# Moving sums, copies, scores and one store in a fused attention and feed-forward kernel

## The chip, the cores and the metric

One core of a Trainium2 chip runs the kernel in one launch. The metric is the device time of one execution in microseconds (us); less is better. The runs before took 310.1, 310.56 and 311.13; the median is 310.56.

## The reference

Eight batches of attention with 8 heads, 576 positions and 64 dimensions per head, with a decay bias, then a feed-forward layer (512 to 2048 to 512) over all 4608 tokens:

```python
scores = scale * np.matmul(q, k.transpose(0, 1, 3, 2))
s_pos = np.maximum(s, 0.0)
cum = np.cumsum(s_pos, axis=-1)
bias = -(cum[:, :, :, None] - cum[:, :, None, :])
scores = np.where(causal, -1000000000.0, scores + np.minimum(bias, 0.0))
attn = softmax(scores)
x = np.matmul(attn, v)      # then heads side by side: 4608 x 512
h = x @ w_in
out = (0.5 * h * (1.0 + erf(h / np.sqrt(2.0)))) @ w_out
```

## The kernel before

Batches pass through attention one after the other, and tokens pass through the feed-forward layer in nine chunks of 512. Chunk c's layers run on TensorE (PE) between the attention steps of batch c + 1, all in an order that is written out by hand: every engine executes its instructions in the order in which the code issues them, and waits only for data and for buffers. PE's results go to a few named PSUM slots: "m0" and "m1" of one bank each, "x", "y" and "z" of two banks each; a slot that is taken again waits for the readers of what it held.

Per batch, `tr_two`, `tr_one` (PE) transpose q and k into `qkT`, and VectorE or ScalarE copy the result out of PSUM; from batch 3 on DMA transposes do this. `sc_mm` makes the scores of a pair of heads in two units and ScalarE takes their exponential into `P`; `mask` multiplies by a triangle. `sc_first` is the form for batch 0: the mask is added by PE (`ident_bf` times `off_bf`), and the bank's first matmul opens the group. The decay is a weight `wb` = exp(cum) on the keys' side: `scale_v` (VectorE) scales V by it into `vv`, and PE forms denominators (`av_d`, weights `wb`) and sums (`av_o`, weights `vv`) with the same `P`. Then ScalarE takes a reciprocal by logarithm and exponential (`ln`), and VectorE multiplies into `xT`. For batch 0 this goes by halves of chunk 0, `av_first` and `x_first`; afterwards by `av_main` and `av_tails`.

`l1_first` and `l1_item` are layer 1 (`h_ps`, two 128-wide tiles at a time), followed on ScalarE by the activation into `gT`. Layer 2 is `l2_item` for chunk 0 (16 accumulating matmuls into `o_ps`, copied out and stored). For later chunks it is `prod`, seven products in place of eight, which need sums of `gT` (`sums`, into `gs`) and of the weights (`weight_sums`, into `w_sums`), all on VectorE. `fill` issues matmuls whose result nobody reads. `put` and `put_one` store a block of the output.

What stands around the places that change: batch 0's prefix sum `weights_dve` runs after the first tiles, and its transposes `weights_mm` after those of the first keys; `av_first(1, ...)` stands behind the first eight matmuls of layer 1; in chunk 1, `after(f2)` issues the transposes of batch 2 behind the chunk's sums; in the last chunk the store of the last block but one is issued by ScalarE:

```python
put(c, 1, 0, pb, m1, queue=nc.scalar)
for i in range(2):
    prod(c, 2, p2[i], more=True, subs=(i,), at=i)
    put_one(c, i, p2[i][:, 0])
```

Of the kernel before, what the change touches and what calls it, by code (L numbers as in the profile page):

```python
# [19 lines left out]
def kernel(  # L20
# [10 lines left out]
    nc = tc.nc  # L31
    fp32 = mybir.dt.float32
# [16 lines left out]
    FT = dff // 128  # L49
# [205 lines left out]
    def weight_sums(i):  # L255
# [8 lines left out]
        nc.vector.tensor_tensor(t[3], b21, t[1], op=ALU.subtract)  # L264

    cum = const.tile([64, S], fp32, name="cum")

    def weights_dve():
        s_pos = work.tile([64, S], fp32, tag="w64", bufs=1, name="s_pos")
        nc.scalar.activation(s_pos, s_sw, func=AF.Relu)  # L270
        nc.vector.tensor_tensor_scan(s_pos, one, s_pos, 0.0, op0=MULT, op1=ALU.add)
        nc.vector.tensor_scalar(cum, s_pos, s_pos[:, 287:288], None, op0=ALU.subtract)

# [174 lines left out]
    def sc_first(p, u, slot):  # L448

        if u == 0:  # L450
            P_of[0, p] = work.tile([128, 2, PW], bf16, tag="P", bufs=4, name="P")
        P = P_of[0, p]
        s_ps = bank(slot, [128, 2, 512], fp32, "sc_ps")
        for n_part, (jt, i0, n, off) in enumerate(UNITS[u]):
            for e in range(2):
                nc.tensor.matmul(
                    s_ps[:, e, off : off + n],
                    lhsT=qkT[0][e * 64 : e * 64 + 64, 1, p, jt * 128 : jt * 128 + 128],
                    rhs=qkT[0][e * 64 : e * 64 + 64, 0, p, i0 : i0 + n],
                    start=n_part == 0, stop=False, skip_group_check=True,  # L460
                )
        for e in range(2):
            nc.tensor.matmul(
                s_ps[:, e].rearrange("p (g c) -> p g c", c=256)[:, :, 0:128], lhsT=ident_bf,
                rhs=off_bf.unsqueeze(1).to_broadcast([128, 2, 128]),
                start=False, stop=True, skip_group_check=True,
            )
            if u == 1:
                nc.tensor.matmul(
                    s_ps[:, e, 448:512], lhsT=ident_bf, rhs=off_bf[:, 0:64],  # L470
                    start=False, stop=True, skip_group_check=True,
                )
        nc.scalar.activation(
            P[:, :, UO[u] : UO[u] + UW[u]], s_ps[:, :, : UW[u]], func=AF.Exp, scale=scale
        )
# [67 lines left out]

    def av_first(c, qds, d_ps, oo):

        for qd in qds:
            av_mm(0, qd, d_ps[:, qd], None, PART[c])
            for t in range(2):
                av_mm(0, qd, oo[:, qd, t], t, PART[c])

# [67 lines left out]

    def l2_item(c, sub, f0=0, f1=FT, slot=None, eng=None):

        gT = gT_of[c]
        if f0 == 0:
            if slot is None:
                o_of[c, sub] = bank(M[sub % 2], [128, KO * 128], fp32, "o_ps")
            elif slot in M:
                o_of[c, sub] = bank(slot, [128, KO * 128], fp32, "o_ps")
            elif sub == 2:
                two = bank(slot, [128, 2, KO * 128], fp32, "o_ps")
                o_of[c, 2], o_of[c, 3] = two[:, 0], two[:, 1]
        o_ps = o_of[c, sub]  # L630
        for ft in range(f0, f1):
            nc.tensor.matmul(  # L632
                o_ps, lhsT=gT[:, ft, sub * 128 : (sub + 1) * 128],
                rhs=w_out_r[:, ft], start=(ft == 0), stop=(ft == FT - 1),
            )
        if f1 < FT:
            return
        o_sb = work.tile([128, KO * 128], fp32, tag="osb", bufs=4, name="o_sb")
        copy(eng or nc.vector, o_sb, o_ps)
        r0 = c * NB + sub * 128  # L640
        nc.sync.dma_start(out=out[r0 : r0 + 128], in_=o_sb)
# [58 lines left out]

    def put(c, t, n, ps_, plus, eng=None, subs=slice(0, 2), queue=nc.sync):

# [6 lines left out]
        queue.dma_start(  # L709
            out=out[r0 : r0 + HC, n * HC : n * HC + HC].rearrange("(s p) x -> p s x", p=128)[:, subs],  # L710
# [70 lines left out]
    oo0 = bank(X, [128, 2, 2, 256], fp32, "av_o")  # L781
    av_first(0, (0, 1), d0, oo0)
    x_first(0, (0, 1), d0, oo0, ln0)
    sc_first(3, 1, Z)
    fill(f_ps, 6)
    scale_v(0, STS[4:5], nc.vector)
    for k0 in (0, 2):
        l1_first(0, 0, k0, k0 + 2)
    d1 = bank(M[1], [128, 2, 256], fp32, "av_d")
    oo1 = bank(X, [128, 2, 2, 256], fp32, "av_o")  # L790
    av_first(1, (0, 1), d1, oo1)
    for qd in range(2):
        x_first(1, (qd,), d1, oo1, ln1)
    l1_first(0, 1, 0, KO)
    for k0 in (0, 2):
# [19 lines left out]
    for c in range(NCH):  # L815
        nb = c + 1

        def after(f2):
            if c == 0:
# [48 lines left out]
        if c == 0:  # L868
# [43 lines left out]
        elif nb < B:  # L912
            exp_set()
            m1, u2, u3, u4, pa, pb, x, y, z = products(c, order[c])
            order[nb] = (y, x, z)
            sums(c, 7, 8, (0, 1))
            prod(c, 1, pa)
            nc.vector.tensor_copy(m1, pa)
            sums(c, 7, 8, (2,))
            sc_mm(nb, 0, (z, x))  # L920
            sc_mm(nb, 1, (y,))
# [60 lines left out]
        else:  # L982
# [188 lines left out]
```

## Time and profile before

| | |
|---|---|
| median of the runs | 310.56 us |
| profiled execution, its own time | 311.02 us |
| its span, first to last instruction | 309.1 us |
| granted PE clock, mean | 0.997 |
| busy: PE, VectorE (DVE), ScalarE (ACT) | 298.9, 229.2, 227.5 us |

In a timeline row stand the start and the length in us, the engine, the line in the code, the operation, output<-input by the program's names, shapes and count; in brackets the idle time before it and what ended it. PEld is PE's loading of weights, SPq, ACTq and POOLq are the queues from which DMAs are issued. Ends of matmuls are modelled: one is shown some 0.27 us long for 256 columns, but the next starts 0.11 later.

### The profile page before, as it was taken

To read this page: it belongs to the slowest core of one execution; us is meant where nothing else is said; L and a number is where in the kernel's file an instruction comes from. 1 tells how busy PE (TensorE), PEld (TensorE's weight loads), DVE (VectorE), ACT (ScalarE), POOL (GpSimd) and SP (SyncE) were. 2 spreads that over 40 slices of the span, in tenths; PEclk is the share of its full clock that TensorE was granted. 3 is DMA by queue.
4 is the path that set the end of the run, shared out by engine and by line. 5 is a ranking of instruction groups with operands and counts; after the bars stand their busy time and mean duration, and the time that the engine had idled before them with its cause. 6 is when DMAs were issued, how large, how long until landed. Compare 5 with 4: busy or idle time off the path is not lost.

```text
span 309.1 us, 8419 instructions
## 1 busy us (share of the span) xinstructions
PE 298.9 (97%) x3544; PEld 192.3 (62%) x3544; DVE 229.2 (74%) x513; ACT 227.5 (74%) x293; POOL 72.8 (24%) x97
## 2 busy tenths in 40 slices
PE   7999999999999999999999999999999999999992
PEld 2565444545894578458854885488547854874581
DVE  5659268978699769996997699778977874554650
ACT  3869757867887788879877987798788879565500
POOL 8583447510002520171017201630000000000000
PEclk9999999999999999999999999999999999999998
DMA  7999999997027994799699996997540220030013
GB/s 114 224 217 207 206 233 235 227 185 92 2 72 172 141 170 116 169 149 161 123 155 149 166 133 149 148 161 142 131 90 2 70 70 1 2 123 13 3 40 105
DMA packets 111692, 39.16 MB, mean 127 GB/s; under 512 B 95360, under 2 KB 109696, under 8 KB 111648
## 3 DMA queue, kind: packets, MB, share of 16 engines
q0 software_dynamic: 54992, 17.18, 50.2%
q1 hardware_dynamic: 56096, 20.86, 33.6%
q8 instruction: 29, 0.48, 0.7%
q10 hardware_dynamic: 560, 0.52, 0.5%
q14 instruction: 15, 0.12, 0.2%
HBM read 36.85 MB, written 9.44 MB: 150 GB/s over the span
## 4 chain that ended last, share of the span: by engine, by line
PE 75%; DMA 18%; POOL 3%; issue 1%; ACTq 1%; ACT 0%; DVE 0%; POOLq 0%
PE h_ps L608 33%; PE pb L682 14%; PE pa L682 9%; DMA raw_v<-in_v_dram 6%; DMA w_out_r<-in_moe_w_out_dram 5%; PE pd L682 5%; PE pe L682 5%; PE sc_ps L438 4%; DMA tok<-in_q_dram 4%; DMA w_in_r<-in_moe_w_in_dram 3%; PE av_o L497 3%; PE av_d L497 1%; POOL raw_v L198 1%; POOL tok L172 1%; PE av_t L497 1%
## 5 line engine op out<-in xcount | busy, mean ns | idle before, releaser
L608 PE MATMUL h_ps<-xT,w_in_r 128*128 128x512 bf16 x560 | 123.5, 379 | 0.0
L608 PEld LDWEIGHTS <-w_in_r 128*128 128x128 bf16 x560 | 54.2, 98 | 62.9
L614 ACT ACTIVATE gT<-h_ps 128x1024 f16<-128x1024 f32 x61 | 60.6, 1022 | 30.4 <-PE h_ps L608 30.4
L444 ACT ACTIVATE P<-sc_ps 128x1024 bf16<-128x1024 f32 x56 | 53.7, 1024 | 8.2 <-PE sc_ps L438 8.2
L682 PEld LDWEIGHTS <-gs 128*128 128x128 f16 x512 | 48.6, 98 | 7.6 <-issue 1.3
L172 POOL DMA_DIRECT2D tok<-in_q_dram x25 | 21.3, 852 | 109.6 <-DMA qkT<-tok 106.5
L664 DVE TENSOR_TENSOR gs<-gT 128x512 f16<-128x512 f16 (+1 forms) x80 | 29.1, 365 | 23.5 <-ACT gT L614 20.6
L210 DVE TENSOR_REDUCE amx<-qkT 128x2 f32<-128x1152 bf16 x32 | 42.2, 1344 | 0.1
L682 PEld LDWEIGHTS <-gT 128*128 128x128 f16 x384 | 37.0, 98 | 6.7 <-ACT gT L617 0.2
L682 PE MATMUL pa<-w_out_r,gT 128*128 128x256 f16 x256 | 31.6, 273 | 0.0
L682 PE MATMUL pb<-w_sums,gs 128*128 128x256 f16 x256 | 30.7, 273 | 0.0
L481 DVE TENSOR_TENSOR P<-P,tri_bf 128x512 bf16<-128x512 bf16 x56 | 22.3, 419 | 10.0 <-ACT P L444 10.0
L228 DVE TENSOR_TENSOR vv<-raw_v,wb 128x512 bf16<-128x512 f32 (+1 forms) x40 | 25.6, 682 | 1.2 <-DMA raw_v<-in_v_dram 1.2
L534 DVE TENSOR_TENSOR xT<-av_o,ln 128x256 bf16<-128x256 f32 (+2 forms) x64 | 21.3, 384 | 3.4 <-ACT ln L513 2.5
L172 POOL DMA_DIRECT2D tok<-in_k_dram x25 | 21.5, 859 | 2.2 <-DMA fk<-in_k_dram 1.1
L217 ACT ACTIVATE junk<-xT 128x2048 bf16<-128x2048 bf16 x9 | 17.1, 1898 | 0.1
L438 PE MATMUL sc_ps<-qkT 64*128 64x256 bf16 x280 | 16.3, 249 | 0.5 <-ACT P L444 0.5
L513 ACT ACTIVATE ln<-ln,lnb 128x256 f32<-128x256 f32 (+1 forms) x31 | 16.0, 515 | 1.0
L664 DVE TENSOR_TENSOR gs<-gs,gT 128x512 f16<-128x512 f16 (+1 forms) x40 | 14.9, 372 | 1.4
L497 PEld LDWEIGHTS <-vv 128*32 128x32 bf16 x784 | 15.1, 96 | 0.8 <-issue 0.6
L497 PE MATMUL av_o<-P,vv 128*32 128x256 bf16 (+1 forms) x528 | 15.5, 256 | 0.0
L632 PE MATMUL o_ps<-w_out_r,gT 128*128 128x512 f16 x64 | 15.4, 380 | 0.0
(130 smaller groups left out, 341.6 us busy)
## 6 DMA issues: line engine op xcount, KB each, us to landing
out_dram<-o_sb SPq DMA_DIRECT2D x34, 256.0 KB, 2.3
raw_v<-in_v_dram SPq DMA_DIRECT2D x20, 256.0 KB, 10.1
raw_v<-in_v_dram POOLq DMA_DIRECT2D x12, 256.0 KB, 9.0
tok<-in_q_dram POOLq DMA_DIRECT2D x20, 128.0 KB, 8.0
tok<-in_k_dram POOLq DMA_DIRECT2D x20, 128.0 KB, 9.4
w_out_r<-in_moe_w_out_dram POOLq DMA_DIRECT2D x4, 512.0 KB, 14.7
fq<-in_q_dram POOLq DMA_DIRECT2D x6, 288.0 KB, 8.3
fk<-in_k_dram POOLq DMA_DIRECT2D x6, 288.0 KB, 9.6
```

The source lines that it names most:

```text
L172: nc.gpsimd.dma_start(out=t[:n_st, i].rearrange("p (h d) -> p h d", d=D), in_=bass.AP(tensor=src.tensor, offset=src.offset + b * H * S * D ...
L210: nc.vector.tensor_reduce(amx[:, b * NP + p], qkT[b % 2][:, :, p, :S], axis=AX, op=ALU.max, apply_absolute_value=True)
L228: eng.tensor_tensor(vb[:n_st, st], t[:n_st, st], wb[:n_st, st, b * H : b * H + H].unsqueeze(2).unsqueeze(3).to_broadcast([n_st, H, 2, D // ...
L438: nc.tensor.matmul(s_ps[:, e, off : off + n], lhsT=qkT[b % 2][e * 64 : e * 64 + 64, 1, p, jt * 128 : jt * 128 + 128], rhs=qkT[b % 2][e * 6 ...
L444: nc.scalar.activation(P[:, :, UO[u] : UO[u] + UW[u]], s_ps[:, :, : UW[u]], func=AF.Exp, scale=scale)
L481: eng.tensor_tensor(d, d, tri_bf.unsqueeze(1).unsqueeze(1).to_broadcast([128, 2, 2, 128]), op=MULT)
L497: nc.tensor.matmul(o[g * 32 : g * 32 + 32, lo : lo + n], lhsT=(wb[:, jt, b * H + h : b * H + h + 1].to_broadcast([128, 32]) if t is None e ...
L534: nc.vector.tensor_tensor(xT[:, 2 * qd + t, x0 : x0 + hi - lo], o[t][:, c * 256 + lo : c * 256 + hi], ln[:, c * 256 + lo : c * 256 + hi], ...
L608: nc.tensor.matmul(h_ps[:, i, :], lhsT=w_in_r[:, ko, ft * 128 : (ft + 1) * 128], rhs=xT[:, ko, c * NB % XW : c * NB % XW + NB], start=(ko ...
L614: nc.scalar.activation(gT_of[c][:, f2 * 2 : f2 * 2 + 2, :], h_ps, func=AF.Gelu)
L664: nc.vector.tensor_tensor(*todo[i][:3], op=todo[i][3])
L682: nc.tensor.matmul(ps_[:, sub - at], lhsT=lhs[:, j, sub * 128 : sub * 128 + 128], rhs=rhs[:, j], start=not more and j == 0 and sub == subs ...
```

## The change

Seven edits, none of which changes what is computed. (1) The prefix sum of the decay is issued ahead of the small tiles, its transposes ahead of those of the first keys and into slot z; two fills go. (2) `sc_first` issues the mask's matmuls ahead of the scores. (3) `av_first` can do denominators and sums apart; denominators of both quadrants go first. (4) Batch 0's second half goes ahead of all of layer 1, and two of six fills go. (5) In chunk 1 the transposes and their copies go ahead of the chunk's sums, one set of weight sums moves by one step, and two scalings of V move into layer 2. (6) At the end of chunk 0 the scores of pair 3 are split around a block of four layer-2 matmuls, and that block's output copy moves behind the second half. (7) The store of the last block but one is issued by SyncE.

```diff
+    cum = const.tile([64, S], fp32, name="cum")
+    s_pos = work.tile([64, S], fp32, tag="w64", bufs=1, name="s_pos")
+    nc.scalar.preload_act_table_set("natural_log_exp_and_others")
+    nc.scalar.activation(s_pos, s_sw, func=AF.Relu)
+    nc.vector.tensor_tensor_scan(s_pos, one, s_pos, 0.0, op0=MULT, op1=ALU.add)
     ident_bf = const.tile([128, 128], bf16, name="ident_bf")
     nc.vector.tensor_copy(ident_bf, ident)
+    nc.vector.tensor_scalar(cum, s_pos, s_pos[:, 287:288], None, op0=ALU.subtract)
...
-    exp_set()
-    weights_dve()
...
     fill(f_ps, 2)
+    weights_exp(weights_mm(Z))
     t_k = [bank(m, [128, FR, 64], bf16, "tr_ps") for m in M]
...
-    fill(bank(Y, [128, 512], fp32, "fill"), 2)
-    weights_exp(weights_mm(X))
     sc_first(0, 0, Y)
...
-    av_first(0, (0, 1), d0, oo0)
+    av_first(0, (0, 1), d0, None, (None,))
+    av_first(0, (0, 1), None, oo0, (0, 1))
     x_first(0, (0, 1), d0, oo0, ln0)
     sc_first(3, 1, Z)
-    fill(f_ps, 6)
+    fill(f_ps, 4)
     scale_v(0, STS[4:5], nc.vector)
-    for k0 in (0, 2):
-        l1_first(0, 0, k0, k0 + 2)
     d1 = bank(M[1], [128, 2, 256], fp32, "av_d")
+    av_first(1, (0, 1), d1, None, (None,))
     oo1 = bank(X, [128, 2, 2, 256], fp32, "av_o")
-    av_first(1, (0, 1), d1, oo1)
+    av_first(1, (0, 1), None, oo1, (0, 1))
     for qd in range(2):
         x_first(1, (qd,), d1, oo1, ln1)
-    l1_first(0, 1, 0, KO)
+    for f2 in range(2):
+        l1_first(0, f2, 0, KO)
...
+            if c == 1 and 2 <= f2 < 6:
+                tr_two(2, f2 // 2 - 1, f2 % 2, (nc.vector, nc.scalar))
             if f2 in (1, 3, 5):
                 sums(c, f2 - 1, f2 + 1)
...
-                if f2 == 1:
+                if f2 == 2:
                     weight_sums(3)
-                if 2 <= f2 < 6:
-                    tr_two(2, f2 // 2 - 1, f2 % 2, (nc.vector, nc.scalar))
-                if f2 in (3, 4, 5):
-                    scale_v(2, STS[2 * f2 - 6 : 2 * f2 - 4], nc.vector)
+                if f2 in (4, 5):
+                    scale_v(2, STS[2 * f2 - 8 : 2 * f2 - 6] if f2 == 4 else STS[2:3], nc.vector)
...
-            sc_mm(1, 3, (z, x))
+            sc_mm(1, 3, (z,))
+            l2_item(c, 1, 12, later=True)
+            sc_mm(1, 3, (x,), 1)
+            l2_out(c, 1, nc.scalar)
...
-            l2_item(c, 1, 12, eng=nc.scalar)
             l2_item(c, 2, 12, eng=nc.scalar)
...
+            if c == 1:
+                scale_v(2, STS[3:4], nc.vector)
             sums(c, 7, 8, (0, 1))
             prod(c, 1, pa)
             nc.vector.tensor_copy(m1, pa)
             sums(c, 7, 8, (2,))
+            if c == 1:
+                scale_v(2, STS[4:5], nc.vector)
...
-            put(c, 1, 0, pb, m1, queue=nc.scalar)
+            put(c, 1, 0, pb, m1)
```

PE's order in the opening, from the last fill on, before (the first row of each kind; `h_ps` is layer 1's PSUM tile):

```order
L405 MATMUL fill<-xT 128x512
L590 LDWEIGHTS w_in_r
L590 MATMUL h_ps<-xT,w_in_r 128x256
...
L497 LDWEIGHTS wb
L497 MATMUL av_d<-P,wb 32x128
...
L497 LDWEIGHTS vv_102
L497 MATMUL av_o<-P,vv_102 32x128
```

And after the change, PE at the same place:

```order
L403 MATMUL fill<-xT 128x512
L495 LDWEIGHTS wb
L495 MATMUL av_d<-P,wb 32x128
...
L495 LDWEIGHTS vv_102
L495 MATMUL av_o<-P,vv_102 32x128
...
L587 LDWEIGHTS w_in_r
L587 MATMUL h_ps<-xT,w_in_r 128x256
```

The eight matmuls of layer 1 that stood ahead of the second half now stand behind it, and all denominators stand ahead of all sums.

VectorE's rows in chunk 1's layer 1, before, from the last of four weight sums to the third copy (`tr_ps` is the transposes' PSUM tile, `gs` the chunk's sums, `vv` the scaled V):

```order
L264 TENSOR_TENSOR w_sums<-w_out_r,w_sums 128x512
L399 COPY qkT_104<-tr_ps 128x576
L664 TENSOR_TENSOR gs_1285<-gT 128x512
L664 TENSOR_TENSOR gs_1286<-gs_1285,gT 128x512
L664 TENSOR_TENSOR gs_1287<-gT 128x512
L399 COPY qkT_104<-tr_ps 128x576
L228 TENSOR_TENSOR vv_102<-raw_v,wb 128x512 x2
L399 COPY qkT_104<-tr_ps 128x576
```

And after the change, VectorE at the same place:

```order
L397 COPY qkT_104<-tr_ps 128x576
L267 TENSOR_TENSOR w_sums<-w_out_r 128x512
L268 TENSOR_TENSOR w_sums<-w_out_r 128x512
L269 TENSOR_TENSOR w_sums<-w_out_r,w_sums 128x512
L270 TENSOR_TENSOR w_sums<-w_out_r,w_sums 128x512
L397 COPY qkT_104<-tr_ps 128x576
L664 TENSOR_TENSOR gs_1279<-gT 128x512
L664 TENSOR_TENSOR gs_1280<-gs_1279,gT 128x512
L664 TENSOR_TENSOR gs_1281<-gT 128x512
L397 COPY qkT_104<-tr_ps 128x576
```

The first copy now stands ahead of the four weight sums, the second ahead of the three sums of the chunk that were in front of it.

ScalarE's rows at the end of the program, before (`pa` are the PSUM tiles of the last two half blocks):

```order
L991 TENSOR_LOAD bad
L709 DMA out_dram<-o_sb 128x2x256
L697 COPY o_sb<-pa_4936 128x256
L699 DMA out_dram<-o_sb 128x256
L697 COPY o_sb<-pa_4937 128x256
```

And after the change, ScalarE at the same place:

```order
L995 TENSOR_LOAD bad
L697 COPY o_sb<-pa_4930 128x256
L699 DMA out_dram<-o_sb 128x256
L697 COPY o_sb<-pa_4931 128x256
L699 DMA out_dram<-o_sb 128x256
```

The store of the block before (L709) has left ScalarE's order; it stands on SyncE as the third of its last stores.

More of the change, by code (lines that the diff above doesn't have):

```diff
@@ L264, in weight_sums @@
         nc.vector.tensor_tensor(t[3], b21, t[1], op=ALU.subtract)
[L266 to L272, printed above, removed]
     def weights_mm(slot):
@@ L453, in sc_first @@
         s_ps = bank(slot, [128, 2, 512], fp32, "sc_ps")
+        for e in range(2):
+            nc.tensor.matmul(
+                s_ps[:, e].rearrange("p (g c) -> p g c", c=256)[:, :, 0:128], lhsT=ident_bf,
+                rhs=off_bf.unsqueeze(1).to_broadcast([128, 2, 128]),
+                start=True, stop=False, skip_group_check=True,
+            )
+            if u == 1:
+                nc.tensor.matmul(
+                    s_ps[:, e, 448:512], lhsT=ident_bf, rhs=off_bf[:, 0:64],
+                    start=False, stop=False, skip_group_check=True,
+                )
         for n_part, (jt, i0, n, off) in enumerate(UNITS[u]):
@@ L459, in sc_first @@
                     rhs=qkT[0][e * 64 : e * 64 + 64, 0, p, i0 : i0 + n],
[L460 to L471, printed above, removed]
+                    start=False, stop=n_part == len(UNITS[u]) - 1, skip_group_check=True,
                 )
@@ L542, with av_first @@
     ]
-    def av_first(c, qds, d_ps, oo):
+    def av_first(c, qds, d_ps, oo, what=(None, 0, 1)):
         for qd in qds:
-            av_mm(0, qd, d_ps[:, qd], None, PART[c])
-            for t in range(2):
-                av_mm(0, qd, oo[:, qd, t], t, PART[c])
+            for t in what:
+                av_mm(0, qd, d_ps[:, qd] if t is None else oo[:, qd, t], t, PART[c])
     def x_first(c, qds, d_ps, oo, ln):
@@ L617, in l1_item, with l2_item @@
                 nc.scalar.activation(gT_of[c][:, f2 * 2 + i, :], h_ps[:, i], func=AF.Gelu)
-    def l2_item(c, sub, f0=0, f1=FT, slot=None, eng=None):
+    def l2_item(c, sub, f0=0, f1=FT, slot=None, eng=None, later=False):
         gT = gT_of[c]
@@ L635, in l2_item, with l2_out @@
             )
-        if f1 < FT:
-            return
+        if f1 == FT and not later:
+            l2_out(c, sub, eng)
+    def l2_out(c, sub, eng=None):
         o_sb = work.tile([128, KO * 128], fp32, tag="osb", bufs=4, name="o_sb")
-        copy(eng or nc.vector, o_sb, o_ps)
+        copy(eng or nc.vector, o_sb, o_of[c, sub])
         r0 = c * NB + sub * 128
@@ L699, in put_one, with put @@
         nc.scalar.dma_start(out=out[r0 : r0 + 128, 0:HC], in_=o_sb)
-    def put(c, t, n, ps_, plus, eng=None, subs=slice(0, 2), queue=nc.sync):
+    def put(c, t, n, ps_, plus, eng=None, subs=slice(0, 2)):
         o_sb = work.tile([128, 2, HC], fp32, tag="osb", bufs=4, name="o_sb")
@@ L708, in put @@
         r0 = c * NB + t * HC
-        queue.dma_start(
+        nc.sync.dma_start(
             out=out[r0 : r0 + HC, n * HC : n * HC + HC].rearrange("(s p) x -> p s x", p=128)[:, subs],
```

## The prediction

> **What bounds the kernel now.** I read the page's busy table first, then busy time by stage (start:end and length; busy us and instructions of PE, PEld, DVE, ACT and POOL; PE's granted clock; DMA share and GB/s), then the timeline of each stage in which TensorE (PE) is not full.
>
> ```profile
> PE 298.9 (97%) x3544; PEld 192.3 (62%) x3544; DVE 229.2 (74%) x513; ACT 227.5 (74%) x293; POOL 72.8 (24%) x97
> ...
> 17.60:25.20 7.60, 7.27 (x128) 5.36 (x121) 4.23 (x6) 5.20 (x9) 5.54 (x10) 1.00 1.17 212
> 51.10:58.70 7.60, 6.64 (x168) 4.17 (x168) 7.23 (x19) 7.33 (x14) 6.03 (x7) 1.00 1.38 215
> 58.70:75.60 16.90, 16.18 (x217) 7.76 (x211) 14.81 (x30) 11.32 (x15) 2.24 (x3) 1.00 1.43 170
> 75.60:301.30 225.70, 225.70 (x2441) 153.91 (x2440) 174.93 (x408) 173.44 (x222) 33.63 (x40) 1.00 0.75 103
> ```
>
> PE is busy 97% of the span. From 75.60 to 301.30 it is busy for all of 225.70 us: nothing in that stretch can be gained but by fewer matmuls, and the change takes away none there. What can move lies in four other places: the opening of batch 0 (up to 25.2), the end of chunk 0 (51 to 59), chunk 1's layer 1 (59 to 76) and the last stores (after 301.3). In the first three PE runs on without a break after the place, so a microsecond won there arrives at 75.6, and from there at the end, unless a later wait takes it. I go through them in that order.
>
> **The opening.** Here, PE's order around the two halves of chunk 0 and what runs beside it:
>
> ```profile
> 15.04 2.16 ACT L473 ACTIVATE P<-sc_ps 128x1024 bf16<-128x1024 f32 x2
> 16.51 0.35 PE L497 MATMUL av_d<-P,wb 128*32 128x256 bf16 x8
> 17.01 0.34 PE L497 MATMUL av_d<-P,wb 128*32 128x256 bf16 x8
> 17.40 0.60 ACT L512 ACTIVATE ln<-av_d 128x512 f32<-128x512 f32 x1 [0.20 <-PE av_d L497]
> 18.03 0.72 ACT L513 ACTIVATE ln<-ln,lnb 128x512 f32<-128x512 f32 x1
> 18.23 1.46 PE L405 MATMUL fill<-xT 128*128 128x512 bf16 x6
> 18.66 1.00 ACT L473 ACTIVATE P<-sc_ps 128x1024 bf16<-128x1024 f32 x1
> 18.79 1.29 DVE L555 TENSOR_TENSOR xT<-av_o,ln 128x512 bf16<-128x512 f32 x2 [1.36 <-ACT ln L513]
> 19.53 1.20 PE L590 MATMUL h_ps<-xT,w_in_r 128*128 128x256 bf16 x8
> 20.66 0.40 PE L497 MATMUL av_d<-P,wb 128*32 128x128 bf16 x12
> 20.89 0.61 PE L497 MATMUL av_o<-P,vv 128*32 128x128 bf16 x24
> 22.10 1.05 PE L590 MATMUL h_ps<-xT,w_in_r 128*128 128x256 bf16 x8
> 23.48 1.91 PE L590 MATMUL h_ps<-xT,w_in_r 128*128 128x256 bf16 x16 [0.33 <-DVE xT L555]
> ```
>
> Before, the second half's sums stand behind eight layer-1 matmuls (19.53), its reciprocal and product come late, and PE waits 0.33 for them at 23.48. The new order, step by step. Denominators of both quadrants go first: the second group ends at about 16.51 + 0.35 + 0.17 = 17.03 instead of 17.35, so ScalarE's logarithm waits no more for PE but for the exponential that ends at 17.20. It starts 0.16 sooner, and VectorE's two products (18.79 to 20.08) end at about 19.9. PE does its four remaining fills until 18.23 + 4 x 0.22 = 19.1 and the denominators of the second half (24 matmuls, two groups of 0.22) until about 19.65, since the last ones need the exponential that now ends at 19.5. The second half's sums write the bank that the products read, so they start at 19.95: that wait is new, and behind it on PE stand all of layer 1. They take four groups of 0.22, to 20.83. Then layer 1: 16 matmuls take 1.91 and 8 take 1.05, so 0.108 each; 32 and a change of kind take 3.57, to 24.40. Meanwhile logarithm, exponential and product of the second half end at about 22.4, before its first use at 22.65 and 23.5, so the 0.33 is gone. Before, layer 1's halves ended at 23.48 + 16 x 0.108 = 25.21. **Gain 0.81.** Ends: 0.64 if the products do not come sooner than 20.08, 1.1 if nothing is waited for at the bank.
>
> The rest of the opening (the prefix sum moved ahead, two fills gone, the mask's matmuls ahead of the scores) I cost at nothing:
>
> ```profile
> 11.65 0.37 PEld L390 LDWEIGHTS <-fk 64*64 64x64 bf16 x36 [0.20 <-DMA fk<-in_k_dram]
> ...
> L105 POOL DMA_DIRECT2D fk<-in_k_dram x1: 748/748/748, 3.5 to 3.5; - x1
> ...
> DMA to landing us min/median/max: 8.1/8.1/8.1
> ...
> 1.48 4.45 PE L405 MATMUL fill<-xT 128*128 128x512 bf16 x10 [1.48 <-DVE xT L120]
> ```
>
> The scores of pairs 0 and 1 do start some 0.5 sooner. But the second quadrant's keys are issued at 3.5 and land 8.1 later, at 11.6, and PE takes them up at 11.65 already. A PE that is 0.4 ahead waits there 0.4 longer, and goes on as before. Range: -0.1 to +0.1.
>
> [...]
>
> **Scores split around a block** (end of chunk 0):
>
> ```profile
> 51.12 0.39 PE L438 MATMUL sc_ps<-qkT 64*128 64x256 bf16 x4
> 52.03 0.40 PE L438 MATMUL sc_ps<-qkT 64*128 64x256 bf16 x6 [0.52 <-ACT P L444]
> 52.36 1.90 PE L632 MATMUL o_ps<-w_out_r,gT 128*128 128x512 f16 x8
> 55.61 0.21 DVE L486 TENSOR_TENSOR P<-P,tri_bf 128x128 bf16<-128x128 bf16 x1
> 58.21 1.41 DVE L534 TENSOR_TENSOR xT<-av_o,ln 128x256 bf16<-128x256 f32 x4
> 58.43 0.32 PE L497 MATMUL av_t<-P,vv 128*32 128x64 bf16 x18 [0.45 <-issue]
> ```
>
> The second group of pair 3's scores waits for a bank that ScalarE still reads. With four layer-2 matmuls between (half of the x8 row, 0.9 us), the bank is free when PE comes. Six such matmuls take 0.33 (52.03 to 52.36), so four take some 0.23 and the second group could have started at 51.35: the wait is 0.68 from start to start (0.52 shows as idle, the rest is the drain of the first group). The two more changes of kind cost about 0.1 each, an estimate: 0.48 net. ScalarE's order stays as it is, because the output copy is issued behind the exponential as before; it ends no sooner. Is something late next? The last mask ends at 55.82, and PE, 0.48 earlier, wants it at 55.94. Layer 1 of chunk 1 starts at 58.2 and reaches its second half of contraction at 59.9; the product that feeds it ends at 59.62. Both fit narrowly. **Gain 0.48**; lower end 0.3 if one of them is missed. The 0.45 at 58.43 waits for nothing the profile shows, in the middle of equal matmuls; I leave it, and should it go, the gain is up to 0.9.
>
> **Chunk 1's copies ahead of its sums**:
>
> ```profile
> 66.06 0.75 DVE L399 COPY qkT<-tr_ps 128x576 bf16<-128x576 bf16 x1
> 66.21 0.10 PEld L390 LDWEIGHTS <-fk 64*64 64x64 bf16 x1 [0.42 <-issue]
> 66.86 0.48 PE L390 MATMUL tr_ps<-ident_bf,fk 64*64 64x64 bf16 x36 [0.58 <-DMA tok<-in_q_dram]
> 68.51 0.75 DVE L399 COPY qkT<-tr_ps 128x576 bf16<-128x576 bf16 x1
> 69.10 0.57 PEld L390 LDWEIGHTS <-fq 64*64 64x64 bf16 x36 [0.42 <-issue]
> 69.31 0.48 PE L390 MATMUL tr_ps<-ident_bf,fq 64*64 64x64 bf16 x36
> 79.08 0.42 DVE L481 TENSOR_TENSOR P<-P,tri_bf 128x512 bf16<-128x512 bf16 x1 [0.81 <-ACT P L444]
> ```
>
> PE has its weights at 66.21 and transposes at 66.86; at 69.10 and 69.31 likewise. Each time it starts 0.05 after VectorE's copy of the transposes before (66.06 + 0.75, 68.51 + 0.75): two banks serve all four groups. The label "DMA tok" names a transfer that these matmuls do not read, so I take the copy as releaser. Ahead of the first copy stand four weight sums, ahead of the second three sums of chunk 1. With the copies in front, both banks are free before PE asks, ScalarE's copy included. **Gain 0.65 + 0.21 = 0.86.** What stands behind now: the weight sums, the chunk's sums and two scalings of V slide later by up to 0.75. None of these is read before layer 2, and the two scalings that move into layer 2 (about 0.67 each) lie once before ScalarE's last activation, once in VectorE's idle 0.81 at 79.08. So they cost nothing; if that cover were missing, 0.67 at most.
>
> **SyncE's store**:
>
> ```profile
> 301.14 1.91 PE L682 MATMUL pa<-w_out_r,gT 128*128 128x256 f16 x16
> 302.07 0.43 ACTq L709 DMA_DIRECT2D out_dram<-o_sb  x1
> 302.69 0.37 ACT L697 COPY o_sb<-pa 128x256 f32<-128x256 f32 x1 [9.71 <-PE pa L682]
> 303.10 1.04 ACTq L699 DMA_DIRECT2D out_dram<-o_sb  x1
> 304.26 0.37 ACT L697 COPY o_sb<-pa 128x256 f32<-128x256 f32 x1 [1.19 <-issue]
> ```
>
> Of the last 16 matmuls the first eight end near 302.3, but ScalarE issues the store of the block before until 302.50 and copies at 302.69. With that store on SyncE, whose queue is empty then, the copy starts at about 302.4: 0.3 sooner. Then comes the issue of 1.04, for which the second copy (ready at 303.05) waits until 304.26. If it keeps its length, 0.3 is all. If it is long only because a store stood ahead of it in ScalarE's queue, it takes 0.43 like that one, and 0.96 is won. I take 0.3, because the same instruction in the same place took 1.04. [...]
>
> **The sum.** 0.81 + 0.48 + 0.86 + 0.30 = 2.45. The profiled execution took 311.02, so 308.57 of its own; it stands 0.46 above the median of the runs, 310.56, against which the result is measured: **308.1 us**, 0.8% less. A difference under 0.3% (0.93 us) can't be told from none here.
>
> **The rivals.**
>
> A. The waits of chunk 1 are a transfer's, as the label says. For it: the profile's own name. Against it: the 0.05 after the copies, twice. Then 0.86 is lost: 1.59 gained, 309.0.
>
> B. Both uncertain extras come: the 0.45 at 58.43 goes, and the last issue shortens by 0.66. 2.45 + 1.11 = 3.56, 307.0. For it speaks that neither names a partner it waits for; against it, that neither is touched.
>
> C. Most of it is given back: PE comes early to stages that hang on ScalarE and VectorE (7.33 and 7.23 of 7.60 busy at 51 to 59), so the opening's 0.81 and the split's 0.48 are waited away there. 1.16 is left, 309.4; with the tail or a part of chunk 1 missing too, no change that can be told. Against it: those engines' work there starts from PE's results and so moves with it.
>
> [...]
>
> **How the numbers follow.** Forecast 0.62, A 0.10, B 0.12, C 0.11, D 0.05. The forecast's own range is 307.6 to 308.6 (its terms' lower ends, 0.64 + 0.3 + 0.86 + 0.3, and its upper ones without B). The range that leaves out two in ten reaches over A and most of B: 306.8 to 309.6. Faster by over 0.3%: forecast, A, B and a third of C, 0.87. Within 0.3%: the rest of C, 0.08. Slower: D, 0.05.
>
> **What the profile after would show.** Opening: layer 1's 512-wide matmuls start near 24.4 instead of 25.2; PE waits for the products at 19.9 and not at 23.5; the keys' transposes stay at 11.65. End of chunk 0: no wait of the second score group for ScalarE. Chunk 1: PE's transposes follow their weights within 0.1. Full PE from about 73.4 on. Tail: the first copy 0.1 after its matmuls; the issue behind it, 1.04 or 0.4, tells B. I am wrong if PE waits anew for a mask or a product at 55 to 60, if the transposes still wait without a copy ahead of them, or if the granted clock drops before 20.

## The result, and the profile after

| | before | after |
|---|---|---|
| median of 7 runs | 310.56 us (310.05 to 311.13) | 308.73 us (307.95 to 309.09) |
| profiled execution, its own time and span | 311.02, 309.1 | 307.95, 306.1 |

The ratio is 0.9938, 95% interval 0.992 to 0.9955: 1.83 us less. The two profiled executions differ by 3.07, more than the medians, since the profile after is of the quickest of its seven runs and that of before is of one of the slower ones. What follows reads places from the profiles, one execution of each kernel, and takes the worth of a part from the runs as well. "Lead" is how much sooner PE comes to a place than in the profile of before, and a "pair" is one weight load of PE with its matmul.

The stages after (start:end and length; busy us and instructions of PE, PEld, DVE, ACT, POOL; PE's granted clock, DMA share, GB/s), cut where PE passes the same points of the program as in the rows of before:

```profile
17.60:25.20 7.60, 7.33 (x128) 5.62 (x123) 5.84 (x8) 5.72 (x9) 5.43 (x9) 1.00 1.17 211
50.40:57.70 7.30, 6.88 (x168) 4.04 (x168) 6.94 (x18) 7.17 (x14) 5.18 (x6) 1.00 1.23 211
57.70:73.60 15.90, 15.49 (x207) 7.40 (x210) 14.08 (x29) 11.28 (x15) 3.17 (x5) 1.00 1.62 187
73.60:299.30 225.70, 224.97 (x2428) 154.03 (x2441) 176.20 (x410) 173.45 (x222) 33.63 (x40) 1.00 0.78 104
```

Full PE starts at 73.6 instead of 75.6 and again lasts 225.7 (its 0.73 less of busy time is matmul records missing from the trace: x2428 beside x2441 weight loads). The clock stays at 1.00 in these stages. The opening and the end of chunk 0, PE's rows with the two copies that matter there:

```profile
19.49 0.62 PE L495 MATMUL av_d<-P,wb 128*32 128x128 bf16 x24
19.93 1.18 PE L495 MATMUL av_o<-P,vv 128*32 128x128 bf16 x48
21.05 3.67 PE L587 MATMUL h_ps<-xT,w_in_r 128*128 128x256 bf16 x32
24.55 1.67 PE L605 MATMUL h_ps<-xT,w_in_r 128*128 128x512 bf16 x6
...
53.48 1.12 ACT L395 COPY o_sb<-o_ps 128x512 f32<-128x512 f32 x2
54.65 1.02 PE L629 MATMUL o_ps<-w_out_r,gT 128*128 128x512 f16 x4 [0.22 <-ACT o_sb L395]
56.94 0.68 DVE L397 COPY o_sb<-o_ps 128x512 f32<-128x512 f32 x1
57.42 0.30 PE L495 MATMUL av_t<-P,vv 128*32 128x64 bf16 x15 [0.20 <-issue]
57.68 3.61 PE L605 MATMUL h_ps<-xT,w_in_r 128*128 128x512 bf16 x15
```

The second half's sums start at 19.93 and layer 1's 512-wide matmuls at 24.55 instead of 25.22: 0.67. Pair 3's second score group waits for nothing any more, and batch 1's sums start 1.15 sooner, at 53.04 (54.19 before). But a wait that was not there follows at 54.65: the last matmuls of block 3 stand behind ScalarE's copy of block 2, with which they share a tile. And layer 1 of chunk 1 starts 0.06 after VectorE's copy of block 3 ends (56.94 + 0.68). At 57.68 the lead is 1.01. Then chunk 1 and the tail:

```profile
65.19 0.48 PE L388 MATMUL tr_ps<-ident_bf,fk 64*64 64x64 bf16 x36
65.60 1.69 PE L605 MATMUL h_ps<-xT,w_in_r 128*128 128x512 bf16 x7
67.43 0.48 PE L388 MATMUL tr_ps<-ident_bf,fq 64*64 64x64 bf16 x36
73.54 1.91 PE L682 MATMUL pa<-w_out_r,gT 128*128 128x256 f16 x16
...
299.14 1.91 PE L682 MATMUL pa<-w_out_r,gT 128*128 128x256 f16 x16
300.22 0.37 ACT L697 COPY o_sb<-pa 128x256 f32<-128x256 f32 x1 [9.23 <-PE pa L682]
300.62 0.38 ACTq L699 DMA_DIRECT2D out_dram<-o_sb  x1
301.18 0.37 ACT L697 COPY o_sb<-pa 128x256 f32<-128x256 f32 x1 [0.58 <-PE pa L682]
301.58 0.48 ACTq L699 DMA_DIRECT2D out_dram<-o_sb  x1
```

No transposes wait for a copy, and the products start at 73.54 (75.43 before): the lead is 1.89. In the tail the issue of 1.04 has become 0.38, and the last copy comes 0.40 after the start of the last matmul (300.78) instead of 1.48 (302.78).

### The profile page after: what moved, and what is told of

It is laid out like the page before. It is cut to its first block, busy times and chain, and to the rows that moved or that the text cites. A ratio compares the mean times of both kernels' runs of the same rounds, so it can differ in the third digit from the quotient of the medians.

```text
span 306.1 us, 8393 instructions
## 1 busy us (share of the span) xinstructions
PE 296.3 (97%) x3519; PEld 191.7 (63%) x3540; DVE 229.1 (75%) x513; ACT 227.3 (74%) x293; POOL 74.2 (24%) x97
## 4 chain that ended last, share of the span: by engine, by line
PE 92%; DMA 3%; ACT 2%; issue 1%; POOL 1%; ACTq 0%; POOLq 0%
PE h_ps L605 39%; PE pb L682 14%; PE pa L682 9%; PE pd L682 5%; PE pe L682 5%; PE sc_ps L436 5%; PE o_ps L629 4%; PE av_o L495 4%; DMA fk<-in_k_dram 3%; PE av_d L495 1%; ACT P L442 1%; PE tr_ps L388 1%; PE h_ps L587 1%; PE av_t L495 1%; PE fill L403 1%
## 5 line engine op out<-in xcount | busy, mean ns | idle before, releaser
L605 PE MATMUL h_ps<-xT,w_in_r 128*128 128x512 bf16 x541 | 122.0, 380 | 1.0 <-issue 0.2
L682 PE MATMUL pb<-w_sums,gT 128*128 128x256 f16 x128 | 15.3, 273 | 0.0
```

What stands on the lines that cost most here:

```text
L605: nc.tensor.matmul(h_ps[:, i, :], lhsT=w_in_r[:, ko, ft * 128 : (ft + 1) * 128], rhs=xT[:, ko, c * NB % XW : c * NB % XW + NB], start=(ko ...
L682: nc.tensor.matmul(ps_[:, sub - at], lhsT=lhs[:, j, sub * 128 : sub * 128 + 128], rhs=rhs[:, j], start=not more and j == 0 and sub == subs ...
```

## The experiments

Each ran beside new runs of the kernel before; ratios are against those. A ratio is not that of the two medians, from which it differs by up to 0.002 here.

**1 to 4: each part alone.** On the kernel before:

```
e1  after(f2), c == 1:  + tr_two(2, ...) ahead of sums(...), weight_sums(3) and scale_v(2, ...) later
e2  + sc_mm(1, 3, (z,)); l2_item(c, 1, 12, later=True); sc_mm(1, 3, (x,), 1); l2_out(c, 1, nc.scalar)
e3  - put(c, 1, 0, pb, m1, queue=nc.scalar)    + put(c, 1, 0, pb, m1)
e4  + av_first(0, ..., (None,)) for both quadrants first; av_first(1, ...) ahead of l1_first; fill(f_ps, 4)
```

> The kernel before with chunk 1's part of the change alone: VectorE's and ScalarE's copies of batch 2's transposes stand ahead of chunk 1's sums, the weight sums and three scalings of V move back. Theory (the copy releases the transposes): the two waits of PE in chunk 1's layer 1 (0.65 and 0.21) are gone, full PE starts 0.8 to 0.9 sooner than in the kernel before (74.6 to 74.8 instead of 75.6 in the profile), and the time falls by 0.86, ratio 0.997. Rival (a transfer releases them, as the label of the wait says; the waits went in the changed kernel because everything else stood earlier): the waits stay in the trace, the time falls by under 0.2.

Measured: 309.79 against 310.44, ratio 0.9972 (0.9945 to 0.9999). From layer 1 of chunk 1 to the first product PE takes 15.87 instead of 16.74: 0.87, and the two transposes that waited, now at 66.10 and 68.34, follow the matmuls before them at once:

```profile
66.10 0.48 PE L390 MATMUL tr_ps<-ident_bf,fk 64*64 64x64 bf16 x36
68.34 0.48 PE L390 MATMUL tr_ps<-ident_bf,fq 64*64 64x64 bf16 x36
```

The copies release them, as the theory said; the transfer named by the label does not. In the times the gain is only just clear of none.

> The kernel before with the split of pair 3's scores alone (four layer-2 matmuls between its two groups, their output copy behind the second exponential). Theory: PE's 0.52 of idle time for ScalarE at the second group goes (0.48 from start to start), but the last four layer-2 matmuls of block 3 then wait for ScalarE's copy of block 2, as they do at 54.65 in the changed kernel, and give back 0.25 to 0.3: layer 1 of chunk 1 starts 0.2 to 0.35 sooner, time lower by about 0.25, which the times alone can hardly tell from none. Rival: the new wait comes of the opening's head start and not of the split; then the split alone gains its whole 0.48.

Measured: 310.42 against 310.44, ratio 0.9993 (0.9969 to 1.0018). The wait for ScalarE's copy of block 2 is there without the opening's lead, and layer 1 follows VectorE's copy of block 3 (57.77 + 0.68) within 0.05:

```profile
55.47 1.02 PE L632 MATMUL o_ps<-w_out_r,gT 128*128 128x512 f16 x4 [0.22 <-ACT o_sb L397]
57.77 0.68 DVE L399 COPY o_sb<-o_ps 128x512 f32<-128x512 f32 x1
58.50 1.67 PE L608 MATMUL h_ps<-xT,w_in_r 128*128 128x512 bf16 x6
```

From the opening's 512-wide matmuls to layer 1 of chunk 1 PE takes 33.13 here and in the changed kernel, 33.47 in the profile of before, but also 33.14 and 33.17 in e3 and e4, which do not split the scores. The 0.48 is won and given back within 5 us.

> The kernel before with the last block but one stored by SyncE instead of ScalarE, nothing else. Theory (ScalarE's issue of the next store is long because a 256-row store stands ahead of it in the same queue): the first of the two last stores issues in about 0.4 instead of 1.04, the second copy follows its matmuls at once, and the time falls by about 1.0, ratio 0.997. Rival 1: the length of that issue changes from execution to execution and had nothing to do with the queue; then the copy comes 0.3 sooner and the time falls by 0.3. Rival 2: the store on SyncE lands later, and the end of the kernel waits for it: no gain.

Measured: 309.59 against 310.44, ratio 0.997 (0.9943 to 0.9998).

```profile
302.00 0.37 ACT L697 COPY o_sb<-pa 128x256 f32<-128x256 f32 x1 [9.23 <-PE pa L682]
302.40 0.38 ACTq L699 DMA_DIRECT2D out_dram<-o_sb  x1
302.96 0.37 ACT L697 COPY o_sb<-pa 128x256 f32<-128x256 f32 x1 [0.59 <-PE pa L682]
```

The issue takes 0.38 here and in the changed kernel, and 0.97 to 1.04 in the four profiles (before, e1, e2, e4) in which the 256-row store stands ahead of it on ScalarE. The later runs agree: 0.97 in e5 and 0.75 in e7 with that store ahead, 0.38 in e6 and e8 to e12 without it. So it is the queue, and rival 1 falls; the length with the store ahead does vary. Counted from the start of PE's last matmul, the last store is issued 1.0 sooner than in e1, e2 and e4 and lands 0.9 sooner (3.0 against 3.9), but the span ends only 0.6 sooner (5.33 against 5.93 to 5.96, and 6.32 in the profile of before): 2.3 instead of 2.0 pass between the last landing and the end, and why was not tried. In the later runs it is 5.98 and 6.02 with the store on ScalarE (e7, e5) and 5.29 to 5.33 with it on SyncE (e6, e8 to e11); e12 has 5.79, its very last issue being 0.83 long, for a reason that stays open.

> The kernel before with batch 0's second-half sums ahead of layer 1 and 4 fills instead of 6, the first 16 us as in the kernel before. Theory: PE waits at the bank near 19.9 instead of 23.5, the first 512-wide layer-1 matmul starts at 24.4 to 24.6 instead of 25.2, and as PE does not stop until 51 the head start of 0.65 to 0.8 is there at the scores of pair 3 (50.4 instead of 51.1) and, through ScalarE's wait there, which moves with it, at the end: time lower by 0.7. Rival: it is waited away between 51 and 59, where ScalarE and VectorE are nearly full; then layer 1 of chunk 1 starts at 58.5 or later, and the time is lower by under 0.3.

Measured: 310.92 against 310.44, ratio 1.0001 (0.9974 to 1.0029): no gain, and by another way than the rival's.

```profile
19.13 0.62 PE L497 MATMUL av_d<-P,wb 128*32 128x128 bf16 x24
19.62 0.90 PE L497 MATMUL av_o<-P,vv 128*32 128x128 bf16 x40
21.98 0.35 PE L497 MATMUL av_o<-P,vv 128*32 128x256 bf16 x8 [1.46 <-issue]
22.26 3.67 PE L589 MATMUL h_ps<-xT,w_in_r 128*128 128x256 bf16 x32
25.77 0.38 PE L607 MATMUL h_ps<-xT,w_in_r 128*128 128x512 bf16 x1
```

In the middle of equal matmuls PE stops for 1.46, for nothing that the profile names. The page's DMA part has a queue of which the prediction made nothing, queue 8 (its kind: packets, MB, share of 16 engines), alike before and after:

```profile
q8 instruction: 29, 0.48, 0.7%
```

29 packets of 16 KB for 3544 recorded pairs of weight load and matmul before and 3540 after: one for 122 on average. That a packet holds 128 pairs is an estimate, from this count and from the places of the pauses. In the opening and at the end of chunk 0, PE's pauses of 0.2 and more without a releaser stand at pairs 354 and 866 of its stream, four times 128 apart (one pair later where the prefix sum's transposes stand ahead), and where PE had to wait it goes on 1.3 to 1.5 after the packet's transfer has ended:

```
                  pair 354: packet's transfer, PE there, goes on     pair 866: the same
before            19.23 to 20.18   21.55   21.56 (no wait)           56.01 to 56.98   57.78   58.43
e1                19.25 to 20.20   21.42   21.60                     55.90 to 56.88   57.65   58.32
e2                19.76 to 20.71   21.61   22.20                     55.73 to 56.71   57.78   58.08
e3                19.28 to 20.23   21.78   21.78 (no wait)           55.89 to 56.87   58.00   58.33
e4                19.55 to 20.50   20.25   21.98                     56.38 to 57.35   58.34   58.70
after             18.53 to 19.48   20.61   20.77                     55.12 to 56.10   57.02   57.42
```

The new order brings PE to pair 354 sooner, but its instructions are not there. The 0.45 at 58.43 before is the same wait. As e7 shows below, PE waits here for more than data and buffers: for its own instructions too. These places have a DMA share of 1.17 and 1.23 (first two stages above) and small matmuls. In the long stretch after 73.6, with a share of 0.78 and larger matmuls, PE is busy throughout; which of the two matters was not tried apart.

**5 and 6: the first part (prefix sum, two fills, mask first), alone and left out.**

```
e5  before, with the diff's hunks 1 to 3 and the fills and weights_exp lines only
e6  after, with those undone
```

> The kernel before with the first part of the change alone: prefix sum moved ahead, two fills gone, mask matmuls ahead of the scores. By the sum of the prediction nothing: the second quadrant's keys land at 11.4 to 11.7 and PE takes them at once, time within 0.2. Theory now (PE's instructions come in blocks of 128 pairs of weight load and matmul over a DMA queue of their own; a block can be used 1.3 to 1.5 after its transfer has ended): the block with pair 354 arrives sooner than in the kernel before if this part is what brings it (its transfer started at 18.5 in the changed kernel and at 19.2 to 19.8 in the kernel before and three parts of the change); the opening does not need it sooner here, so layer 1's 512-wide matmuls start at 25.0 to 25.3 either way. If the transfer starts at 19.2 or later here too, this part is not what brings it.

Measured: 310.39 against 310.39, ratio 0.9996 (0.9973 to 1.0019); the packet's transfer starts at 18.95, layer 1's 512-wide matmuls at 25.45, a little past the range of 25.0 to 25.3. The times show no gain of this part alone, as the prediction said.

> The changed kernel with its first part undone (prefix sum, fills and order of mask and scores as before). Theory (instruction blocks): PE reaches pair 354 at about 20.3, finds the block not there and waits for 1 to 1.7 until 21.6 to 22.0, as in the opening alone; layer 1's 512-wide matmuls start at 25.4 to 25.8, the opening's gain is lost, and the time is 310.5 - 0.3 - 0.9 - 0.6 = 308.7 or some more, 0.5 to 0.8 above the changed kernel run beside it. Rival (the wait of 1.46 in the opening alone was an accident of one execution): layer 1's 512-wide matmuls start at 24.4 to 24.6 and the time equals the changed kernel's.

Measured: 309.42, ratio 0.9957 (0.9929 to 0.9984), against 0.9938 for the changed kernel. Transfer 19.75 to 20.70; PE there at 20.59, goes on at 22.05; 512-wide matmuls at 25.84 instead of 24.55. In these single executions, then, the two halves of the opening, neither with a gain of its own in the times, need each other: with the first the packet comes sooner, and the second uses it. The times don't show it: the difference (0.0019 of the ratio, 0.6 us) is smaller than in this one execution, and the intervals overlap.

**7: the block's end moved.** e4, with `fill(f_ps, 10)` replaced by `fill(f_ps[:, 0:205], 25)`.

> The opening's part alone, with the first ten fills of 512 columns cut into 25 of 205 columns: the same time on PE, 15 instruction pairs more ahead of everything else, so each block's end lies 15 pairs earlier in the program. Theory (instruction blocks): pair 226 is passed at 14.0 to 14.6 instead of 15.8, the block behind pair 354 can be used at about 20.2 instead of 22.0, and PE, which is there at 20.0, waits under 0.5: layer 1's 512-wide matmuls start at 24.3 to 24.7 instead of 25.8. The wait at the tails' sums (58.3 to 58.7 in all kernels so far) goes, since pair 866 now is passed 15 pairs earlier. A new wait of 0.3 to 0.9 comes at pair 610, which now lies behind only 5.1 us of work (near 43). Rival (the wait of 1.46 is for data, or for an engine): it stays at the same place of the program, ahead of the last eight sums, and layer 1 starts at 25.4 or later.

```profile
19.81 0.66 PE L497 MATMUL av_o<-P,vv 128*32 128x128 bf16 x25
20.84 0.62 PE L497 MATMUL av_o<-P,vv 128*32 128x128 bf16 x23 [0.38 <-issue]
24.91 1.46 PE L607 MATMUL h_ps<-xT,w_in_r 128*128 128x512 bf16 x6
```

The wait has moved by exactly 15 matmuls (25 and 23 instead of 40 and 8) with nothing but the count of instructions ahead changed, and again ends 1.51 after its packet (19.34). A wait for data or for an engine would have stayed at its place of the program: the instruction block is shown. The wait at pair 866 is gone. The start of layer 1 missed its range by 0.2, and the new wait at 610 did not come. The times don't follow, though: 310.84, ratio 1.0024 (1.0003 to 1.0045); the profiled execution is the quickest of its twelve, and what the others waited for isn't known.

**8: the copies swapped.** After, with `l2_out(c, 1, nc.scalar)` behind `l2_item(c, 2, 12, eng=nc.scalar)`.

> The changed kernel with ScalarE's output copies of layer 2's blocks 1 and 2 in the other order, so that the copy of block 2, for which PE waits at 54.65, comes first. Both theories: the wait of 0.29 at 54.65 goes. Naive: layer 1 of chunk 1 starts 0.3 sooner (57.4) and so does the end. Instruction blocks: pair 866's block ends its transfer at about 56.1 whatever PE does after 53, PE reaches it 0.3 sooner and waits 0.3 longer, layer 1 starts at 57.6 to 57.7 as before, and the time is that of the changed kernel within 0.1.

Measured: 308.81, ratio 0.9934 (0.9909 to 0.9959). The wait for ScalarE is gone and PE is through pair 867 without one, and still layer 1 starts 33.13 after the opening's 512-wide matmuls:

```profile
PE h_ps L605 <- DVE o_sb L397: 0.6, 1, 0.6
```

No gain, as forecast by the second theory, but for a third reason: VectorE's copy of block 3. Three waits lie one behind the other there (ScalarE's copy, the instruction block, VectorE's copy), and taking one away uncovers the next.

**9 and 10: what brings the packet sooner.** In the changed kernel VectorE's scan stands beside GpSimd's first mask, which then takes 1.40 instead of 0.34, and all loads behind it are issued 1.4 later:

```profile
4.33 1.40 POOL masks.py:199 TENSOR_SCALAR_AFFINE_SELECT ident<-ident 128x128 f32<-128x128 f32 x1
4.30 1.35 DVE L150 TENSOR_TENSOR_SCAN s_pos<-one,s_pos 64x576 f32<-64x576 bf16 x1 [1.83 <-ACT s_pos L149]
```

```
e9   e6  + nc.gpsimd.memset(vv[1][0:64, 0:3], 0.0) ahead of load_v(0, ...)
e10  after, with tensor_tensor_scan and the subtraction for cum moved behind off_bf and memset(wb...)
```

> The changed kernel without its first part (prefix sum, fills, order of mask and scores as before), but with 1.5 us of GpSimd memory fills of a tile not yet in use ahead of the loads of V and weights, so that those are issued at about 6.6 instead of 5.1, as late as in the changed kernel, where VectorE's scan slows GpSimd's masks. Theory (the loads that GpSimd has issued stand ahead of PE's instruction blocks, so issuing them later brings the blocks sooner): the blocks' transfers start near 11.9 and 18.5 to 18.9 instead of 13.3 and 19.8, PE's wait at pair 354 is under 0.5 instead of 1.46, layer 1's 512-wide matmuls start at 24.5 to 25.0 instead of 25.8, and the time is the changed kernel's within 0.4. Rival (what brings the blocks is another piece of the first part): transfers at 13 and 19.5 or later, wait over 1, layer 1 at 25.5 or later.

Measured: 308.41, ratio 0.9925 (0.9909 to 0.9942). But in the profiled execution, the slowest of its six (309.34, the others 307.99 to 308.54), the transfer starts at 19.40, PE waits 1.37 at pair 354 and the 512-wide matmuls start at 25.64. The trace speaks against the theory, the times for it. The edit also did more than was meant: beside GpSimd's memset (5.11 to 6.48) VectorE's copy of the mask took 1.36 instead of 0.23, so the scan began at 6.79 instead of 5.73 and PE waited 0.35 for the prefix sum.

> The changed kernel with VectorE's scan (and the subtraction behind it) put back behind the copies of identity and mask, all else of the first part kept. Theory (the late loads bring the instruction blocks): GpSimd's first mask takes 0.34 again instead of 1.40, the loads of V are issued at 5.1, the block for pair 354 starts its transfer at 19.2 or later instead of 18.5 to 18.9, PE waits there for over 0.7, layer 1's 512-wide matmuls start at 25.1 or later instead of 24.6, and the time is 0.5 to 1 above the changed kernel's. Rival (the two dropped fills or the order of mask and scores bring the blocks): 24.4 to 24.8 and the changed kernel's time.

Measured: 310.60, ratio 0.9999 (0.9987 to 1.0012): with only the scan put back, none of the gain is left in the times.

```profile
20.52 0.99 PE L495 MATMUL av_o<-P,vv 128*32 128x128 bf16 x41
22.79 0.34 PE L495 MATMUL av_o<-P,vv 128*32 128x256 bf16 x7 [1.28 <-issue]
26.57 0.81 PE L605 MATMUL h_ps<-xT,w_in_r 128*128 128x512 bf16 x2
```

The packet starts at 20.54, ends at 21.49, and PE goes on at 22.79. PE also stops in the middle of ten score matmuls at pair 611, two blocks further on, until 46.87, 1.73 after that block's packet (45.14). PE also comes 0.6 later to the first sums (17.17 instead of 16.58), with 0.5 of waiting for the prefix sum on the way. So with the rest of the first part in place a late scan costs the whole gain. That the gain needs an early scan is not shown: e9, without it, has the changed kernel's times. Nor is it shown that the early scan works by the late loads. The profiles with an early packet (18.46 to 18.95: after, e5, e8, e11; e7 and e12 have their blocks' ends elsewhere) have the scan ahead of all loads of V and weights, while it runs beside their issue in e9 (from 6.79) and e10 (from 5.74). In e8 the first load is issued at 5.92, only 0.8 later than before, and the packet is early (18.68); in e9 it is issued at 6.43, and the packet is late. So the delay of the loads alone doesn't decide it in the profiles; whether a scan beside their issue holds them up wasn't tried.

**11 and 12: towards a faster version.**

```
e11  after, weight_sums(2) behind absmax(1, [0]); scale_v(1, STS) ahead of mask(1, 2); l2_out(c, 1) on VectorE
e12  e11, with fill(f_ps[:, 0:256], 20) for fill(f_ps, 10)
```

> The changed kernel with VectorE and ScalarE relieved between 49 and 57: weight sums 2 (1.4 us) move to VectorE's idle time behind the maxima of pair 0 (near 42.4), the five scalings of V stand ahead of pair 2's mask, and VectorE instead of ScalarE copies out layer 2's block 1. Theory (layer 1 of chunk 1 hangs on ScalarE's copies, then logarithms, then VectorE's products and its copy of block 3, which ends at 57.62 in the changed kernel): the logarithm behind the copies starts 0.4 to 0.5 sooner (53.9 to 54.1), the copy of block 3 ends at 57.0 to 57.2, the wait at 54.65 is gone, and layer 1 starts at 57.2 to 57.4, unless the instruction block of pair 867 (usable 57.0 to 57.4) holds it; time 0.2 to 0.4 under the changed kernel, ratio 0.992 to 0.993. Rival (only the instruction block holds it): 57.5 to 57.7 again and no gain.

Measured: 308.53, ratio 0.9933 (0.9917 to 0.995), the changed kernel's time. PE reaches pair 867 at 56.74, with the wait at 54.65 gone, and then:

```profile
56.60 0.33 PE L495 MATMUL av_t<-P,vv 128*32 128x64 bf16 x17
58.08 0.30 PE L495 MATMUL av_t<-P,vv 128*32 128x64 bf16 x15 [1.14 <-issue]
58.31 1.90 PE L605 MATMUL h_ps<-xT,w_in_r 128*128 128x512 bf16 x7
```

Its packet ended at 56.87 and PE goes on 1.21 later. The engines were relieved as meant; the instruction block holds PE instead.

> The kernel with VectorE and ScalarE relieved between 49 and 57, with the first ten fills of 512 columns cut into 20 of 256: the same time on PE, 10 instruction pairs more ahead of everything else. Theory (after the relief only the instruction block of pair 867 holds layer 1 of chunk 1): that block is asked for some 1 us sooner in PE's program, is usable at 56.0 to 57.0, and PE, which gets there at 56.7, waits under 0.4 instead of 1.34: layer 1 starts 32.7 to 33.0 after the first 512-wide matmuls instead of 33.7. In the opening the block is asked for at 15.1 to 15.5 and usable at 20.3 to 21.0, a wait of 0 to 0.7 as before. Time 0.5 to 0.9 under that kernel, 307.6 to 308.1, ratio 0.9905 to 0.992. Rival (the wait of 1.34 is not for the block, or the block comes as late as before): layer 1 starts 33.5 or more after the first 512-wide matmuls and the time stays.

Measured: 309.39, ratio 0.9955 (0.9936 to 0.9974): missed. Layer 1 comes 33.07 after the opening's 512-wide matmuls, the wait at pair 867 is 0.73, but the opening's wait is 0.90 and its 512-wide matmuls start at 25.34. The profiled execution is the slowest of nine (310.28). Moving the blocks' ends moves the wait, but the packet does not follow: its transfer starts 3.3 after PE has come to the block before (15.52), against 2.3 in e11 (16.18). No version beats the changed kernel by more than the intervals.

## Why the prediction was right, and where it was not

308.1 was forecast, 308.73 measured: faster, as forecast, and within the wide range of 306.8 to 309.6, but outside the forecast's own range of 307.6 to 308.6. Of the 2.45 of the sum, 1.83 came. The number lies nearer to rival A's 309.0, whose mechanism e1 rules out. By the steps of the prediction:

- **Opening, 0.81.** 0.67 in the profile. The wait at the bank came at 19.93 (forecast 19.95), the 512-wide matmuls at 24.55 (24.4); the 0.15 between is the 0.16 at pair 355. The new order does in this execution what was forecast, but only where the packet is there in time. In the times the gain is not seen: e4 has none.
- **The rest of the opening, nothing.** True of the part alone (e5). Its reason holds as far as it goes (the second quadrant's keys are taken at 11.62, as before), but it followed one transfer only and not the packets of instructions: without the first part PE goes on 1.3 later in the opening (e6, one execution), and with the scan alone put back the opening ends 2.0 later and the gain is gone (e10). How the scan acts stays open, and e9's times speak against its being needed.
- **Split scores, 0.48.** Won exactly up to batch 1's sums (from pair 3's first score group to them 50.45 to 53.04, 2.59, against 51.12 to 54.19, 3.07), then given back; the 0.1 for each change of kind in it was an estimate that no row shows alone. In the two profiles 0.34 is left, and only because the profile of before had a wait of 0.65 at pair 866; in the times of e2 no gain can be told. That is rival C, for this part alone. The step named VectorE's mask and product as what could come late next; it left out ScalarE's copy of block 2 and VectorE's copy of block 3.
- **Chunk 1's copies, 0.86.** 0.87. Rival A falls: the copy, not the labelled transfer.
- **SyncE's store, 0.30.** Mis-sized: 0.6 to 1.0. The reading by the queue, half of rival B, was right (its rows give 0.61 for it, 1.04 less 0.43, where the text says 0.66); "the same instruction in the same place took 1.04" was no reason, since its place was behind a store. By the rows 0.66 of issue time is saved (1.04 to 0.38), and not the wait ahead of the copy alone.
- **The 0.45 at 58.43**, left as waiting for nothing, is the instruction block of pair 866 (experiments 4 and 7).
- **Rival D**, slower with 0.05, stood on a fall of PE's clock at small gaps, and no run shows one: in the profile after, the granted clock is 1.00 between 8 and 12, where the gaps are, and stays so up to 303; it is lower only behind PE's last matmul (0.93 from 303 to 306.1), and 0.999 over the span.

In the two profiles 0.67 + 0.34 + 0.88 + 0.11 + 1.0 make the 3.0 of the spans (the 0.11 falls into the full stretch and was not traced). The times tell less. Taken from the ratios of e1 to e5, the copies give 0.87 and the store 0.93, both just clear of none; the split (0.2), the opening's order (none) and the first part (0.1) can't be told from none. Copies and store alone make 1.8, all of the 1.83. So the times do not show that the opening's 0.81 and the split's 0.48, over half of the sum, arrive at the end. The sum came near by some luck: the store gave two to three times its 0.30, which stood in for them.

## What to carry to other kernels

A pause of an engine in the middle of equal instructions, with no releaser, can be its own code, as the 1.46 in e4 was: compare it with the instruction queue's transfers and with the count of instructions. The pauses at pairs 354 and 866 stood where small matmuls ran beside a DMA share of 1.17 and 1.23; what else may bring them was not tried. A part of a change that is costed at nothing should be asked what else it moves, and not only what it does to the wait it stands before: here the place of one scan went with 2 us. A profile is one execution: ask the times of several whether a gain seen there arrives. And after a wait is taken away, list every engine that hands something to the next stage: here three waits lay one behind the other, and each experiment removed only the front one.

## What the hardware showed that was not expected

- Where PE waited for a block of its instructions, it went on 1.2 to 1.6 after the block's transfer had ended (pairs 354 and 866, or one later, of all kernels above; 1.73 at pair 611 of e10). The transfer of the block of pair 354 started 1.9 to 3.8 after PE had come to pair 226 (or 227), the start of the block before.
- A scan of VectorE with two inputs beside GpSimd's mask: 0.34 became 1.40, and the mask ended (5.73) 0.08 after the scan (5.65). In e8 the mask began 0.01 ahead of the scan (4.33) and kept its 0.33; the scan took 1.54 instead of 1.35, and the second mask (from 4.88) 1.09 instead of 0.29. Why the two hold each other up is not shown.
- ScalarE's issue of a 128-row store took 0.97 to 1.04 some 0.6 behind a 256-row store on its queue (0.75 in e7), and 0.38 without.
- One profile of a kernel can stand at the edge of its runs (e7 the quickest of twelve, e9 the slowest of six), with a wait of over 1 us that the others need not have had.
